# Hash attention and an MLP in one kernel: the opening with the first chunk's attention alone, one PSUM bank a head, hash bits compared into place

## The chip, the cores and the metric

The kernel runs on one core of one Trainium2 chip. The metric is device time in microseconds (us), as the median of the runs. Engines are named as in the profile: PE (TensorE, with PEld for its weight loads), DVE (VectorE), ACT (ScalarE), POOL (GpSimd) and SP (SyncE). PEclk is the share of its clock that PE was granted.

## The reference, cut to what matters

There are 4 batches of 8 heads with 768 tokens of 64 dimensions, all in fp32. Each query and each key is hashed to 6 bits, and a query sees only the keys with the same 6 bits. The attention's output is laid out as rows of 512 and goes through a layer norm and an MLP of 2048 hidden units, with a residual.

```python
q_bits = (np.einsum('bhsd,dk->bhsk', q, proj) > 0)          # proj: 64 x 6
k_bits = (np.einsum('bhsd,dk->bhsk', k, proj) > 0)
mask = q_bucket[:, :, :, None] == k_bucket[:, :, None, :]
scores = np.where(mask, scale * q @ k.T, -1e9)
attn = softmax(scores) @ v
x = attn.transpose(0, 2, 1, 3).reshape(B, S, H * D)         # 768 x 512 a batch
out = x + np.maximum(layernorm(x) * g @ w_ch1, 0) @ w_ch2   # 512 -> 2048 -> 512
```

## The kernel before, in words

**Operands.** For each head, `slots` holds queries and keys transposed: rows 0 to 63 are the 64 dimensions in bf16, rows 64 to 69 are the six hash bits as +24 or -24 (batch 0: +0.5 or -0.5, with the operands scaled down to match). One product of 70 rows then gives the score with the mask already in it: each bit that differs takes so much off the score that its exponential is as good as nothing. `vaug` holds the values with a column of ones, so that the value product gives the denominator too. A tiny multiple of the values' sum is added for queries that match no key; for batch 0 it comes into PSUM by "opener" products with the constant tile `epsk` (L431).

**Chunks, units and steps.** Work goes in 12 chunks of 256 queries: three a batch, `(b, t)`. A chunk has four head pairs, and a pair three units of four (head, key block) products each. A unit has a score step (four products, L406, and one exponential of 128x1024 on ACT, L412) and a value step (eight products of 65 columns, L440; the last of a pair divides by the denominator on DVE, L455 and L465). Each chunk then goes through its MLP: norm (L484 to L501: DVE statistics, normalised rows `xn`, and `rs` on POOL), a transpose of `xn` (on PE, L509, for the first two chunks), eight up steps (L522, 8 products of 256 columns each, ReLU by DVE and ACT in turn) and eight down steps (L535, 4 products of 512 columns each).

**Preparation of q and k.** From batch 1 on, transposes and hashes are made from bf16 copies by DMA transposes and 32x32 DVE transposes (`narrow`, `blocks`, `operands`, `hashes`), planned as fillers between attention steps. Batch 0 has no time for that: its heads go through PE (`transposes`, L211: three blocks of q and three of k a head, each block two key or query blocks high). DVE evicts and scales q (L219), ACT evicts k (L221), both to `qkT` in fp32, and `casts` copies them to `slots` (L226 to L231, POOL, ACT or DVE). `hash_pair` hashes two heads' q or k by four products of 32 columns that lie side by side in PE (L306), compares them to bits on DVE (L311), and copies the bits to their rows in `slots` (L322 to L326). Because a transposed block holds the tokens of two key blocks, batch 0's blocks lie in another order in `slots`, which `CMAP` undoes.

**What sets the order.** The first two chunks are written out by hand in `first_two` (L643 to L703): the units of chunk 0 and chunk 1 alternate by head pair, and the dictionary `also` names what is issued between them.

```python
groups = [(0, 0), (0, 1), (1, 0), (1, 1), (2, 0), (3, 0), (2, 1), (3, 1)]
seq = [(n, 3 * j + g) for j, n in groups for g in range(3)]
...
18: [mlp[0][0][1]],
22: [mlp[0][3]],
23: [mlp[0][1][0][1], lambda: nxt.blocks(0, 1, 0), lambda: nxt.blocks(0, 1, 1)],
```

So the first MLP's norm comes behind unit 18, its transpose behind unit 22 and one of its eight up steps behind unit 23; the other seven are fillers of the third chunk's stage. From the third chunk on, `interleave` spreads fillers by their costs between the units: the down steps of the chunk before the previous one, the preparation steps of the string `plan`, and the up steps of the previous one. Every engine takes its own instructions strictly in order; where one waits, all behind it on that engine wait. PE is kept busy ahead of the first data by products with a constant (`keep_awake`, L652: 26, 3 and 10 of them). PSUM holds two score tiles (`ps_sc`, two banks each), two banks for `av` (`ps_av`) and two for everything else (`ps_mm`), among them the batch 0 transposes.

**Loads.** q and k of batch 0 go out on SP and ACT, proj on ACT behind both (L152), values on SP; POOL issues w1 (L559), w2 (L566) and all loads of batch 1.

Of the kernel before, what the change touches and what calls it, by code (L numbers as in the profile page):

```python
# [9 lines left out]
F32 = mybir.dt.float32  # L10
# [10 lines left out]
Q_SCALE = 2.0**-12  # L21

# [6 lines left out]
def kernel(  # L29
# [11 lines left out]
    nc = tc.nc  # L41
# [24 lines left out]
    proj1 = consts.tile([P, 2, 32], F32)  # L66
# [26 lines left out]
    CMAP = [[2 * i + par for par in range(2) for i in range(HC)]] + [list(range(NC))] * (B - 1)  # L93
# [10 lines left out]
    for i in range(2):  # L104
# [12 lines left out]
        tc.tile_pool(name="ps_av", bufs=2, space=bass.MemoryType.PSUM)  # L117
# [18 lines left out]
    def load_half(b, half):  # L136
# [7 lines left out]
        for lo, hi in zip(cuts, cuts[1:]):  # L144
            for nm, src in (("q", q), ("k", k)):
                eng = nc.gpsimd if b == 1 else nc.scalar if nm == "k" and hi - lo == 1 else nc.sync
                eng.dma_start(
                    out=t[nm][:, lo:hi],
                    in_=src[b, h0 + lo : h0 + hi].rearrange("h (p c) d -> p h c d", p=P),
                )  # L150
        if b == 0 and half == 0:
            nc.scalar.dma_start(out=proj1[0:D, 0, 0:n_bits], in_=proj)  # L152

# [19 lines left out]
    class Prep:  # L173
# [24 lines left out]
        def tokens(self, h, par):  # L198

            return self.sl[0:D, h, :, par * HS : (par + 1) * HS]  # L200

        def transposes(self, h, a):

            if a == 0:
                self.qkT[h] = work.tile([P, 2, HS], F32, tag="qkT", bufs=4, name="qkT")
            if h == 1:
                tp = ps_sc.tile([P, 2, 512], F32, tag="sc", name="tpose")[:, 0, 0:HS]
            else:
                tp = ps_mm.tile([P, HS], F32, tag="mm", name="tpose")
            for i in range(HC):  # L210
                nc.tensor.transpose(  # L211
                    tp[:, i * P : (i + 1) * P],
                    self.tiles[h // 4]["qk"[a]][:, h % 4, 2 * i : 2 * i + 2].rearrange(
                        "p c d -> p (c d)"
                    ),
                    identf,
                )
            if a == 0:
                nc.vector.tensor_scalar_mul(self.qkT[h][:, a, :], tp, Q_SCALE)  # L219
            else:  # L220
                nc.scalar.activation(self.qkT[h][:, a, :], tp, AF.Copy)  # L221

        def casts(self, h):
            src = self.qkT[h]
            if h < 2:
                nc.gpsimd.tensor_copy(self.tokens(h, 0), src[0:D])  # L226
                nc.scalar.activation(self.tokens(h, 1), src[D:P], AF.Copy)
            else:
                eng = nc.gpsimd if h in (4, 6) else nc.vector
                eng.tensor_copy(self.tokens(h, 0), src[0:D])  # L230
                nc.vector.tensor_copy(self.tokens(h, 1), src[D:P])  # L231
# [67 lines left out]
        def hash_pair(self, j, a):  # L299

            if a == 0:
                self.pair_bits = work.tile([P, 2, HS], BF16, tag="bits", name="bits")
            bits = self.pair_bits
            hp = ps_mm.tile([P, HS], F32, tag="mm", name="hash")
            for g in range(4):
                nc.tensor.matmul(  # L306
                    hp[32 * g : 32 * (g + 1), :],
                    proj1[:, g % 2, :],
                    self.qkT[2 * j + g // 2][:, a, :],
                )  # L310
            nc.vector.tensor_scalar(  # L311
                bits[:, a, :], hp,
                scalar1=0.0, scalar2=0.5, op0=AOP.is_gt, op1=AOP.subtract,
            )
            if a == 0:
                return
            for g in range(4):
                par = g % 2
                dst = self.sl[D:K1, 2 * j + g // 2, :, par * HS : (par + 1) * HS]
                src = bits[32 * g : 32 * g + n_bits]  # L320
                if g == 2 and j == 0:
                    nc.scalar.activation(dst, src, AF.Copy)  # L322
                elif g == 3:
                    nc.gpsimd.tensor_copy(dst, src)
                else:
                    nc.vector.tensor_copy(dst, src)  # L326

# [60 lines left out]
    def att_units(b, t, x):  # L388
# [3 lines left out]
        q0 = t * CT  # L392
        for j in range(NP):
# [7 lines left out]
            for g, grp in enumerate(groups):  # L401

                def scores(grp=grp, g=g, state=state):
                    sc = ps_sc.tile([P, 4, CT], F32, tag="sc", name="sc")
                    for i, (h, kj) in enumerate(grp):
                        nc.tensor.matmul(  # L406
                            sc[:, i, :],
                            sl[0:K1, h, 1, kj * P : (kj + 1) * P],
                            sl[0:K1, h, 0, q0 : q0 + CT],
# [9 lines left out]
                def values(grp=grp, g=g, state=state, j=j, ha=ha):  # L419
                    if g == 0:  # L420
                        av = ps_av.tile([P, 2, TT, D1], F32, tag="av", name="av")
                        state["av"] = av
                        opens = []
                        if b == 0:
                            opens = (
                                [va[:, ha : ha + 2, c, :] for c in range(NC)]
                                if (t, j) == (0, 0)
# [10 lines left out]
                    for i, (h, kj) in enumerate(grp):  # L438
                        for qi in range(TT):
# [3 lines left out]
                                va[:, h, CMAP[b][kj], :],  # L443
# [29 lines left out]
    def mlp_steps(b, t, x):  # L473
# [56 lines left out]
        def down(i, part):  # L530
# [8 lines left out]
            if part == 3:  # L539
# [5 lines left out]
                    out=out[b].rearrange("(p c) d -> p c d", p=P)[:, CMAP[b][t * TT + i], :],  # L545
# [92 lines left out]
    def head(h):  # L638
        prep.transposes(h, 0)
        prep.transposes(h, 1)  # L640
        prep.casts(h)

    def first_two():  # L643
# [6 lines left out]
        nc.sync.dma_start(out=gbc, in_=moe_g_ln.partition_broadcast(P))  # L650

# [4 lines left out]

        keep_awake(26)
        head(0)
        head(1)
        nc.vector.tensor_copy(proj1[D : 2 * D, 1, 0:n_bits], proj1[0:D, 0, 0:n_bits])  # L660
        keep_awake(3)
        prep.hash_pair(0, 0)
        prep.hash_pair(0, 1)
# [279 lines left out]
```

## Time and profile before

| | |
|---|---|
| runs: median (lowest to highest) | 328.85 us (328.68 to 329.95) |
| profiled execution: span from the first to the last instruction | 329.9 us |
| mean granted PE clock over the span | 0.967 |
| PE busy (PEld) | 310.5 us, 94% (228.3) |
| ACT, DVE, POOL busy | 215.3, 185.9, 84.5 us |
| moved by DMA | 40.93 MB, mean 124 GB/s |
| chain that ended last | PE 79%, DVE 7%, ACT 7%, DMA 2% |

The profile is of one execution; its span agrees with the slowest of the runs and lies 1.05 us above their median. In the groups by line, each row names the line, the engine, the operation, output<-input, the shape and the count, then the busy time and the mean duration of one in ns, then the idle time of the engine just before them and what ended it. In the timeline, a row has the start and the duration in us; a bracket shows the idle time ahead of it and its releaser. In the windows view, each row has a stretch, its length, then the busy time of PE, PEld, DVE, ACT and POOL with the number of instructions, then the granted PE clock, the DMA share and GB/s. PE's records overlap, since products are pipelined: how long a step holds PE is read from start to start, not from the durations.

### The profile page before, as it was taken

What the parts mean: (1) busy time and instruction counts of PE and PEld (TensorE: products, weight loads), DVE (VectorE), ACT (ScalarE), POOL (GpSimd) and SP (SyncE); (2) the same over time, 40 slices, a digit from 0 to 9 for tenths busy, and PEclk for the clock granted to TensorE, in tenths of its full rate; (3) what the DMA queues carried; (4) which work ended last, traced back from release to release, by engine and by line L of the source; (5) the groups of instructions that cost most, each with busy time, mean ns of one, the idle gap of its engine ahead of it and who ended that gap; (6) DMA issues with size and microseconds to landing.
All of it is one profiled execution on the core that took longest, in us unless ns stands there. A gap on an engine that the chain in (4) does not pass through costs nothing.

```text
span 329.9 us, 7872 instructions
## 1 busy us (share of the span) xinstructions
PE 310.5 (94%) x3276; PEld 228.3 (69%) x3276; DVE 185.9 (56%) x406; ACT 215.3 (65%) x269; POOL 84.5 (26%) x105
## 2 busy tenths in 40 slices
PE   7787899799999999999999999989999999999992
PEld 6654568665966967957867868748769678686650
DVE  2688773773394587365497585535533634546420
ACT  5574777643695795787795886897758667573110
POOL 4466424662130524054155030010100200201000
PEclk9999856799999999999999999999999999999999
DMA  7999996576549649669724834020020110200301
GB/s 249 354 223 298 233 295 133 115 158 176 144 98 234 159 155 182 160 129 289 177 59 103 102 75 93 1 67 34 0 66 34 31 67 2 64 34 2 98 3 68
DMA packets 64874, 40.93 MB, mean 124 GB/s; under 512 B 47184, under 2 KB 59728, under 8 KB 64832
## 3 DMA queue, kind: packets, MB, share of 16 engines
q1 hardware_dynamic: 60368, 31.85, 39.3%
q0 software_dynamic: 4096, 8.13, 10.3%
q8 instruction: 27, 0.44, 0.6%
q10 hardware_dynamic: 368, 0.39, 0.3%
q14 instruction: 15, 0.12, 0.1%
HBM read 27.98 MB, written 6.88 MB: 106 GB/s over the span
## 4 chain that ended last, share of the span: by engine, by line
PE 79%; DVE 7%; ACT 7%; DMA 2%; issue 2%; ACTq 0%; SPq 0%; DVEq 0%
PE hp L522 25%; PE o L535 20%; PE sc L406 17%; PE av L440 10%; ACT ex L412 4%; PE hash L275 3%; DVE slots L326 2%; PE hash L306 2%; DMA proj<-in_proj_dram 1%; ACT knat L191 1%; ACT qnat L191 1%; DMA xnT<-xn 1%; PE tpose L211 1%; DVE stats L484 1%; DVE bits L311 1%
## 5 line engine op out<-in xcount | busy, mean ns | idle before, releaser
L412 ACT ACTIVATE ex<-sc,expb 128x1024 bf16<-128x1024 f32 x144 | 159.8, 1114 | 69.4 <-PE sc L406 69.0
L522 PE MATMUL hp<-xnT,w_sb 128*128 128x256 bf16 x768 | 100.5, 276 | 2.4 <-DVE hbuf L129 1.7
L535 PE MATMUL o<-w_sb,hbuf 128*128 128x512 bf16 x384 | 96.0, 379 | 0.2
L406 PE MATMUL sc<-slots 70*128 70x256 bf16 x576 | 91.8, 282 | 2.9 <-DVE slots L326 2.9
L522 PEld LDWEIGHTS <-w_sb 128*128 128x128 bf16 x768 | 72.7, 99 | 12.0 <-issue 2.1
L440 PEld LDWEIGHTS <-ex 128*128 128x128 bf16 x1152 | 55.6, 100 | 22.1 <-ACT ex L412 8.2
L406 PEld LDWEIGHTS <-slots 70*128 70x128 bf16 x576 | 53.0, 100 | 17.5 <-DVE slots L326 2.7
L440 PE MATMUL av<-vaug,ex 128*128 128x65 bf16 x1152 | 61.8, 197 | 2.2 <-ACT ex L412 2.2
L129 DVE TENSOR_SCALAR hbuf<-hp 128x512 bf16<-128x512 f32 x48 | 33.1, 690 | 53.7 <-PE hp L522 52.9
L535 PEld LDWEIGHTS <-hbuf 128*128 128x128 bf16 x384 | 35.5, 97 | 28.6 <-issue 0.6
L500 POOL TENSOR_SCALAR rs<-mv 128x2 f32<-128x2 f32 x12 | 5.7, 477 | 172.6 <-DVE mv L485 172.6
L133 ACT ACTIVATE hbuf<-hp 128x512 bf16<-128x512 f32 x48 | 28.5, 594 | 24.2 <-PE hp L522 24.2
L540 DVE SCALAR_TENSOR_TENSOR x<-o,rs,x 128x512 f32<-128x512 f32 x24 | 17.8, 741 | 36.8 <-PE o L535 36.8
L465 DVE TENSOR_TENSOR x<-x,rc 128x256 f32<-128x256 f32 x36 | 20.6, 573 | 1.0
L486 DVE SCALAR_TENSOR_TENSOR xn<-x,mv,gbc 128x512 bf16<-128x512 f32 x24 | 18.3, 782 | 0.3 <-DVE mv L485 0.3
L457 DVE TENSOR_SCALAR rc<-av 128x4 f32<-128x4 f32 x36 | 5.7, 158 | 18.6 <-PE av L440 18.6
L484 DVE BATCH_NORM_STATS2 stats<-x 128x6 f32<-128x512 f32 x24 | 15.4, 678 | 0.2
L458 DVE TENSOR_TENSOR x<-av,vsum 128x256 f32<-128x256 f32 x36 | 14.9, 414 | 0.0
L330 POOL CAST vaug<-vnat 128x1536 bf16<-128x1536 f32 x8 | 12.0, 1498 | 9.3 <-PE av L440 4.9
L191 ACT ACTIVATE knat<-knat 128x768 f32<-128x768 f32 x16 | 13.5, 846 | 0.0
L191 ACT ACTIVATE qnat<-qnat 128x768 f32<-128x768 f32 x16 | 13.5, 844 | 0.0
L501 POOL TENSOR_TENSOR rs<-rs,mhalf 128x2 f32<-128x2 f32 x12 | 12.7, 1061 | 0.6
(80 smaller groups left out, 207.6 us busy)
## 6 DMA issues: line engine op xcount, KB each, us to landing
out_dram<-x SPq DMA_DIRECT2D x24, 256.0 KB
vnat<-in_v_dram SPq DMA_DIRECT2D x7, 768.0 KB
qnat<-in_q_dram SPq DMA_DIRECT2D x11, 384.0 KB
knat<-in_k_dram SPq DMA_DIRECT2D x11, 384.0 KB
w_sb<-in_moe_w_ch_dram POOLq DMA_DIRECT2D x4, 1024.0 KB, 13.2
slots<-slots SPq DMA_DIRECT2D x6, 384.0 KB
qnat<-in_q_dram POOLq DMA_DIRECT2D x2, 768.0 KB, 12.9
knat<-in_k_dram POOLq DMA_DIRECT2D x2, 768.0 KB, 14.5
```

The costliest lines, as they stand in the source:

```text
L129: nc.vector.tensor_scalar_max(dst, src, 0.0)
L133: nc.scalar.activation(dst, src, AF.Relu if relu else AF.Copy)
L191: nc.scalar.activation(src, src, AF.Square, accum_out=sq[:, a, col : col + 1],)
L406: nc.tensor.matmul(sc[:, i, :], sl[0:K1, h, 1, kj * P : (kj + 1) * P], sl[0:K1, h, 0, q0 : q0 + CT],)
L412: nc.scalar.activation(ex, sc, AF.Exp, bias=expb[:, 1:2] if b else expb[:, 0:1], scale=scale if b else scale / Q_SCALE,)
L440: nc.tensor.matmul(av[:, h - ha, qi, :], state[g][:, i, qi * P : (qi + 1) * P], va[:, h, CMAP[b][kj], :], start=(b > 0 and (g, i, qi) == ( ...
L465: nc.vector.tensor_tensor(xv, num, rc.unsqueeze(3).to_broadcast([P, 2, TT, D]), op=AOP.mult)
L484: nc.vector.bn_stats(stats, x[:, i, :])
L486: nc.vector.scalar_tensor_tensor(xn[:, :, i, :], x[:, i, :].rearrange("p (o d) -> p o d", d=P), mv[:, i, 0:1], gbc.rearrange("p (o d) -> p ...
L522: nc.tensor.matmul(hp[:, i, :], w1_sb[:, dt, nt * P : (nt + 1) * P], st["xnT"][:, dt, :], start=(dt == 0), stop=(dt == ND - 1),)
L535: nc.tensor.matmul(o2, st["h"][:, nt, i * P : (i + 1) * P], w2_sb[:, nt, :], start=(nt == 0), stop=(nt == NH - 1),)
L540: nc.vector.scalar_tensor_tensor(x[:, i, :], o2, st["rs"][:, i : i + 1], x[:, i, :], op0=AOP.mult, op1=AOP.add,)
```

## The change

- The first chunk's twelve units now come first, alone, with all of batch 0's transposes, casts and hashes between them; then the second chunk's twelve, with the whole norm, transpose and all eight up steps of the first chunk's MLP between them. The third chunk's stage no longer has seven of these up steps.
- A head's three k blocks and the one q block that the first chunk needs are transposed to one PSUM bank and evicted by one instruction with the square root of the old scale (2^-6 for both). The other two q blocks come later, for two heads together (`late_transposes`).
- A head is hashed by one product of 64 columns over 512 (its two column groups hold the bits of the two stacked blocks), and the compares on DVE write the bits directly into `slots`. `hash_pair` and its copies go.
- `ps_av` has one bank each of two names, `av0` and `av1`. The transposes use `av1`, and the first chunk's `av` tiles all use `av0`; later chunks alternate.
- All four pairs of the first chunk open with six products of `vaug` instead of one of `vsplit` (before: the first pair alone).
- proj is loaded ahead of the second head's k; the 3 and 10 wake products go; `CMAP` goes, since blocks are found by `key_block` and `query_blocks`.

```diff
-        ps_av ... tc.tile_pool(name="ps_av", bufs=2, space=bass.MemoryType.PSUM)
+        ps_av ... tc.tile_pool(name="ps_av", bufs=1, space=bass.MemoryType.PSUM)
...
+        def transposes(self, h, engine):
+            tp = ps_av.tile([P, 4, P], F32, tag="av1", name="tpose")
+            t = self.tiles[h // 4]
+            for i in range(HC + 1):
+                src, c = (t["k"], 2 * i) if i < HC else (t["q"], 0)
+                nc.tensor.transpose(
+                    tp[:, i, :],
+                    src[:, h % 4, c : c + 2].rearrange("p c d -> p (c d)"),
+                    identf,
+                )
+            self.scaled(h, tp, engine)
...
+        def scaled(self, key, tp, engine):
+            self.qkT[key] = work.tile([P, 4, P], F32, tag="qkT", bufs=4, name="qkT")
+            if engine is nc.scalar:
+                nc.scalar.activation(self.qkT[key], tp, AF.Copy, scale=HALF_SCALE)
             else:
+                engine.tensor_scalar_mul(self.qkT[key], tp, HALF_SCALE)
...
+        def hash_bits(self, key):
+            hp = ps_mm.tile([P, 4, P], F32, tag="mm", name="hash")
+            nc.tensor.matmul(
+                hp[D : 2 * D].rearrange("p c t -> p (c t)"),
+                proj1,
+                self.qkT[key].rearrange("p c t -> p (c t)"),
+            )
+            for par in range(2):
+                r0 = D + 32 * par
+                nc.vector.tensor_scalar(
+                    self.places(key, slice(D, K1), par),
+                    self.as_placed(key, hp[r0 : r0 + n_bits]),
+                    scalar1=0.0, scalar2=0.5, op0=AOP.is_gt, op1=AOP.subtract,
+                )
...
                     if g == 0:
-                        av = ps_av.tile([P, 2, TT, D1], F32, tag="av", name="av")
+                        slot = 0 if (b, t) == (0, 0) else (j + 1) % 2
+                        av = ps_av.tile([P, 2, TT, D1], F32, tag=f"av{slot}", name="av")
...
-                                if (t, j) == (0, 0)
+                                if t == 0
...
         keep_awake(26)
-        head(0)
-        head(1)
-        nc.vector.tensor_copy(proj1[D : 2 * D, 1, 0:n_bits], proj1[0:D, 0, 0:n_bits])
-        keep_awake(3)
-        prep.hash_pair(0, 0)
-        prep.hash_pair(0, 1)
-        keep_awake(10)
+        head(0, act, (pool, dve))
+        dve.tensor_copy(proj1[D : 2 * D, 32 : 32 + n_bits], proj1[0:D, 0:n_bits])
+        head(1, act)
+        bits(0)
+        head(2, act)
+        bits(1)
+        S(0)
+        load_w1()
+        head(3, dve)
         prep.values(0)
+        S(1)
+        bits(2)
+        V(0)
+        head(4, act)
+        S(2)
+        V(1)
+        bits(3)
+        S(3)
+        V(2)
+        head(5, dve)
+        nxt.load(0)
...
+        S(8)
+        late(0, act, in_av)
+        V(7)
+        bits(7)
+        S(9)
+        V(8)
+        load_w2()
+        late_bits(0)
+        S(10)
+        V(9)
+        late(1, act, in_av)
+        prep.split_sums(0)
+        S(11)
+        V(10)
+        late_bits(1)
+        S(12)
+        V(11)
...
+            0: [norm[1]],
+            1: [lambda: late(2, dve, in_mm), lambda: late_bits(2)],
+            2: [lambda: prep.split_sums(1), lambda: nxt.load(1), lambda: nxt.load_v(0)],
+            3: [lambda: late(3, dve, in_mm), lambda: late_bits(3), xtrans],
+            4: [ups[0][1], lambda: nxt.narrow(0, 0)],
+            5: [ups[1][1], lambda: nxt.narrow(0, 1)],
...
+            11: [ups[7][1]],
+        for u in range(n0):
+            S(n0 + u + 1)
+            for f in also[u]:
+                f()
+            V(n0 + u)
...
-        fillers = (mlp[0][1][1:] if n == 2 else []) + [norm]
+        fillers = [norm]
```

Here `head(h, ...)` is the transposes and casts of head h, `bits(h)` its hash, `late(j)` and `late_bits(j)` the same for the two late q blocks of heads 2j and 2j + 1, and `S(u)` and `V(u)` the score and value step of unit u.

## The prediction

> **What bounds the kernel now.** I read the windows view first, cut where the granted clock changes, then the timeline of the opening, then the groups by line.
>
> ```profile
> core 0: us, PE busy (x) PEld busy (x) DVE busy (x) ACT busy (x) POOL busy (x), PEclk, DMA share, GB/s
> 9.50:31.40 21.90, 17.28 (x196) 11.62 (x197) 17.02 (x31) 13.95 (x16) 13.83 (x15) 1.00 1.10 293
> 31.40:34.80 3.40, 3.40 (x25) 3.01 (x25) 2.00 (x5) 1.61 (x2) 1.41 (x2) 0.50 1.24 207
> 34.80:41.60 6.80, 5.76 (x78) 3.28 (x76) 5.62 (x11) 4.95 (x5) 2.92 (x3) 1.00 1.21 249
> 41.60:55.30 13.70, 13.40 (x115) 9.96 (x114) 7.23 (x15) 9.66 (x9) 5.49 (x5) 0.50 0.88 215
> 55.30:62.10 6.80, 5.06 (x58) 4.41 (x57) 6.26 (x12) 6.64 (x13) 1.68 (x2) 1.00 0.67 130
> 62.10:65.50 3.40, 3.40 (x24) 2.58 (x23) 1.60 (x2) 0.34 (x1) 3.24 (x5) 0.50 0.44 94
> 65.50:92.00 26.50, 26.39 (x307) 19.42 (x305) 13.00 (x25) 13.39 (x15) 9.12 (x11) 1.00 0.61 156
> 92.00:302.00 210.00, 207.91 (x2297) 156.46 (x2295) 121.03 (x285) 157.73 (x200) 41.62 (x48) 1.00 0.40 95
> ```
>
> The reader is to see three regions. From 65.5 us to 302 PE is busy over 98% at full clock (PEclk 1.00); nothing in the change touches that work, it only begins earlier or later. Before 65.5 no engine is full, and PE runs at half clock for 3.4, 13.7 and 3.4 us. So the change is decided in the first 92 us: there the third chunk's attention ends, and the eighth up step of the second chunk's MLP beside it. Call S(u) and V(u) the score and value steps of unit u. Before, V(23), the last of the first two chunks, ends at 55.8 with one up step of the first MLP done; the stage of the third chunk lasts 36.2 us, to 92.0.
>
> The half clock comes after idle PE, in the timeline:
>
> ```profile
> 29.01 0.49 PE L211 MATMUL tpose<-identf,qnat 128*128 128x128 f32 x3
> 31.25 0.82 PE L211 MATMUL tpose<-identf,knat 128*128 128x128 f32 x3 [1.75 <-DVE vsplit L358]
> 59.23 0.60 PE L406 MATMUL sc<-slots 70*128 70x256 bf16 x4
> 61.58 1.40 PE L522 MATMUL hp<-xnT,w_sb 128*128 128x256 bf16 x8 [1.74 <-DVE hbuf L129]
> ```
>
> Each wait of 1.75 us is followed by transposes or ups at double length. The changes lie on a grid of 3.41 us (31.38, 34.80, 41.62, 55.28, 62.10, 65.52), which reaches back to 0.66. I summed in each 3.41 us how long PE really streams (spacing of successive starts: score 0.107 us, value 0.028, transpose 0.107). Streaming under 0.41 to 0.50 of a stretch gives half clock in the next; 0.56 and more keeps it full. With a score counted three quarters (70 of 128 rows) one border, 0.42 to 0.44 of full speed, sorts every stretch but the first, and says why 41.6 to 55.3 stayed at half: at half clock attention alone reaches at most 0.415. The stretch with the first ups left it.
>
> **Prices.** From the groups by line and the timeline:
>
> ```profile
> L311 DVE TENSOR_SCALAR bits<-hash 128x384 bf16<-128x384 f32 x8 | 4.4, 553 | 1.8 <-PE hash L306 1.7
> L219 DVE TENSOR_SCALAR qkT<-tpose 128x384 f32<-128x384 f32 x8 | 4.4, 555 | 6.9 <-PE tpose L211 6.8
> L221 ACT ACTIVATE qkT<-tpose 128x384 f32<-128x384 f32 x8 | 3.9, 491 | 4.3 <-PE tpose L211 4.2
> L326 DVE COPY slots<-bits 6x768 bf16<-6x768 bf16 x11 | 7.4, 674 | 0.3
> 10.43 1.47 POOL L330 CAST vaug<-vnat 128x1536 bf16<-128x1536 f32 x1 [0.34 <-DMA vnat<-in_v_dram]
> 11.95 0.84 PE L431 MATMUL av<-vaug,epsk 128*128 128x260 bf16 x6 [0.21 <-POOL vaug L330]
> ```
>
> PE occupancy, start to start: four scores 0.44, eight values 0.24, six openers (L431) 0.68, four transposes 0.43, an up step 0.875, a down step 0.87. An old hash group (four 32-column products side by side, 384 columns) held PE 0.88 us, 0.64 of it streaming. The new hash is one product of 64 columns over 512: 0.64 x 512/384 = 0.85, plus the same 0.24: 1.09 us. No row shows a 64-column product; the ends are 0.85 (no overhead) and 1.3, I take 1.09. Evictions over 512 in place of 384: DVE 0.69 us, ACT 0.60. One head's bits take two DVE compares, 1.38 us; the copies into place (L326, eleven at 0.67 on DVE, four on POOL) go. A POOL cast of 64x512 is 0.55 to 0.8 (820 ns and 1208 ns for 64x768), taken as 0.6.
>
> **Part 1, the first chunk alone.** Work of a head pair on PE: 2 x 0.43 + 2 x 1.09 + 0.68 + 3 x 0.44 + 3 x 0.24 = 5.76 us; ACT has 3 x 1.11 + 0.6, DVE about 4.0, so PE leads. The openers are six instead of one for pairs 1 to 3 (+1.7 us in all), hashing rises from 8 x 0.88 to 12 x 1.09 (+6 us). S(0) starts at about 9.4 as before (9.55): the chain is transpose 3.8, eviction, proj landing at about 6.2, hash, compares to 8.85; proj is issued half a us earlier (head 1's k behind it; its transposes wait for their bank till 5.2 anyway), and the copies and 13 wake products are gone. Behind S(0) stand 4 x 5.76, less three transposes and two hashes done (3.5), plus two late query groups (2 x 1.52), split sums 0.68 and S(12) 0.44: 23.7, so 33.1.
>
> Stall A adds 2.4. POOL's order is now casts of heads 0 to 2, the two w1 issues (0.87 each), casts of head 3, then the values cast. Head 3's casts wait for DVE's scaling, which stands behind head 1's compares (end 10.95): 11.65. Casts to 13.3, vaug to 14.9; V(0) waits for it (before: 11.95). Behind V(0) on PE wait head 4's transposes and S(2), so ACT runs dry too. Small waits, walked link by link, add 0.4 a pair: V(11) ends at 37.1. The av bank of this chunk is single, but the next opener comes a hash and a score after the last value, over 1.2 us against 0.6 of DVE: hidden.
>
> **Part 2, the second chunk with the first MLP.** PE: 12 x 0.44 + 12 x 0.24 + 0.44 + 2 x 1.52 + 0.68 + 0.45 + 8 x 0.875 = 19.8. Stall B: the norm (two times 0.68 + 0.18 + 0.75, and gaps: 3.3 us) stands on DVE ahead of the scaling of late group 2; it starts when chunk 0's last x is written, about 38.7, ends at 42.0, and the late hash, next on PE, starts at 42.8 with PE idle since 39.6: 3.2 us. The next late group waits 1.3, the first up 1.05 for xnT, small waits 0.6. End of V(23): 37.1 + 19.8 + 6.2 = 63.1, 7.3 later than before. DVE's 17.8 us and ACT's 15.1 fit beside. On POOL the loads of the second half of b=1 now stand behind rs, which waits for the norm: issued near 45 instead of 29.3. They land some 14 us later (page), before that stage ends: no cost; if late, narrow and T11 slip, with about 10 us of slack before the fourth chunk. w2 goes out near 32 instead of 25, first used after 63.
>
> **Part 3, the third chunk.** Seven ups leave (6.1 us). What stays is 26.1 us of PE work; the same mix ran at 26.39 of 26.50. I take 27.0, against 36.2: the 1.74 wait and the 3.4 us at half clock (1.7 lost), both in the part of the ups, go with them. Full-clock sum: 63.1 + 27.0 - 92.0 = -1.9.
>
> **The clock.** Stall A puts S(1) and one hash into 10.9 to 14.3: 0.34 of streaming, under the border, so half clock follows; and 4.08 to 7.49 holds 0.42 to 0.46 (0.57 before, with twelve transposes and three wakes). Behind A PE leads, so a half stretch costs 1.7; the mix reaches 0.43 to 0.49 at half clock if the 64-column hash counts fully, so it gets out after about two: 3.4. Stall B costs one such stretch and part of a second, partly hidden under DVE: 2.5. Sum: -1.9 + 5.9 = +4.0. The span of 329.9 becomes 333.9. The profiled span lies 1.05 above the median of the runs (328.85), so 332.9: **333**.
>
> The Trainium skill ("TensorE: Matmul & The Clock Gate", Part 1, and its table of rules) lets the clock fall only after an idle window of about 3.4 us and asks for no gaps over about 3 us. The two gaps of 1.75 us here, each with half clock behind it, speak against it. By that rule stall A would be free, and the second rival below would hold. The same page (Part 4) says that transposes do not count as busy; the stretch 31.4 to 34.8, filled over half by nine fp32 transposes, brought full clock back, so here they count. Without them the opening would be emptier still, toward the first rival.
>
> **Rivals.**
> - Stuck at half clock. If columns count as rows seem to, the hash (64 of 128) counts half; the opening then reaches 0.31 to 0.40 at half clock and stays there, as attention did at 41.6 to 55.3. PE streams 17.7 us from V(0) to V(11); twice that, less 1.5 of absorbed waits, is +16, so with B: 329.9 - 1.9 + 16 + 2.5 - 1.05 = 345.5; leaving halfway, 337. For it: the score's weight. Against: no row shows it of columns. Chance 0.25.
> - The clock holds, and the kernel is faster: 329.9 - 1.9 - 1.05 = 327.0, 324 if the norm's stall is shorter than walked. It decides at the stretch before 14.3: vaug ready by about 13.9 lifts it over the border. For it: stretches of 0.56 stayed full. Against: POOL's order. Chance 0.22.
> - It changes nothing: waits at half clock absorb (V(0) waits for POOL at either clock), 328 to 330. Chance 0.13.
> - Forecast, some half stretches at both stalls, 330 to 336: 0.40.
>
> Only differences over 0.5% (1.64 us) can be told from none. Of the second rival most lies below 327.2: faster 0.18, same 0.20, slower 0.62. The range is 326.5 to 345.
>
> **What would show it.** Right: V(0) behind vaug at 14 to 16 us, PEclk 0.5 from 14.3, a PE gap of about 3 us near 40 ended by DVE qkT, V(23) at 65 to 70, the third stage of about 27 us at full clock. Wrong: hash products spaced far from 1.09; PEclk 1.00 throughout the opening; or a third stage near 36 us, which would mean that its DMAs or squares, not the ups, set it.

## The result and the profile after

| | before | after |
|---|---|---|
| runs beside each other: median (lowest to highest) | 328.9 us (328.68 to 329.95) | **336.94 us** (335.03 to 338.29) |
| ratio of after to before, 95% interval | | 1.0257 (1.021 to 1.0303) |
| profiled execution: span; clock | 329.9 us; 0.967 | 334.0 us; 0.981 |

The ratios leave out slow runs, those over 1.5% above the kernel's fastest; before has seven of them among the 29 runs of the last group below.

The kernel got slower by 8.0 us. The forecast of 333 named the direction; it is too low by 3.9. The two profiled spans differ by 4.1 us, though, close to the 4.0 forecast. So there are two questions: where the 4.1 us are, and where the rest of the 8.0 is.

The windows view of after, cut at its changes of clock and at the ends of V(23) and of the 16th up step:

```profile
core 0: us, PE busy (x) PEld busy (x) DVE busy (x) ACT busy (x) POOL busy (x), PEclk, DMA share, GB/s
1.80:7.20 5.40, 2.78 (x25) 2.36 (x23) 0.89 (x2) 2.09 (x3) 1.44 (x5) 1.00 0.92 283
7.20:14.00 6.80, 5.63 (x12) 2.01 (x12) 1.38 (x2) 1.20 (x2) 2.08 (x4) 0.50 1.06 378
14.00:48.10 34.10, 28.00 (x249) 17.22 (x249) 21.41 (x38) 18.67 (x19) 18.91 (x27) 1.00 0.92 186
48.10:51.60 3.50, 3.50 (x30) 2.65 (x31) 2.19 (x4) 1.11 (x1) 2.67 (x4) 0.51 0.98 186
51.60:68.70 17.10, 15.39 (x187) 12.96 (x186) 10.84 (x19) 11.15 (x12) 6.98 (x6) 1.00 0.80 200
68.70:96.20 27.50, 26.23 (x315) 19.27 (x312) 16.80 (x30) 18.02 (x25) 12.56 (x16) 1.00 0.65 163
96.20:306.00 209.80, 207.78 (x2304) 156.53 (x2302) 120.90 (x285) 157.99 (x201) 42.63 (x49) 1.00 0.40 98
```

The last row is the old last row, 210 us with PE busy 99%: nothing was lost or won there. The third stage is 27.5 us at full clock. All that was lost lies before 68.7. Before, the clock fell late (31.4, 41.6 and 62.1); now it falls at 7.2, in the opening, and at 48.1. The timeline of PE names the waits:

```profile
4.02 0.52 PE L209 MATMUL tpose<-identf,knat 128*128 128x128 f32 x3
4.37 0.27 PE L209 MATMUL tpose<-identf,qnat 128*128 128x128 f32 x1
8.37 0.87 PE L209 MATMUL tpose<-identf,knat 128*128 128x128 f32 x3 [3.73 <-DMA knat<-in_k_dram]
...
9.39 1.97 PE L259 MATMUL hash<-qkT,proj 128*64 128x512 f32 x2
...
19.31 0.84 PE L453 MATMUL av<-vaug,epsk 128*128 128x260 bf16 x6 [2.11 <-POOL vaug L340]
...
47.02 1.07 PE L259 MATMUL hash<-qkT,proj 128*64 128x512 f32 x2 [2.99 <-DVE qkT L234]
53.15 1.07 PE L259 MATMUL hash<-qkT,proj 128*64 128x512 f32 x2 [0.85 <-DVE qkT L234]
56.43 1.03 PE L544 MATMUL hp<-xnT,w_sb 128*128 128x256 bf16 x8 [0.86 <-DVE xnT L535]
```

In the kernel before, head 1's transposes end by 6.2 and the first hash starts at 6.73:

```profile
5.72 0.49 PE L211 MATMUL tpose<-identf,knat 128*128 128x128 f32 x3
6.73 0.71 PE L306 MATMUL hash<-qkT,proj 128*32 128x384 f32 x4 [0.34 <-DMA proj<-in_proj_dram]
```

The reader is to see four things. In after, head 1's transposes wait 3.73 us for k, which the forecast did not have. The transposes and the hash behind that wait take 0.87 and 1.97 us: half clock. The openers of V(0) wait for POOL's cast of the values. And one late group waits 2.99 us for DVE, with half clock behind it (the windows row of 48.1).

Marks from the two traces (first product of V(0), last of V(11) and V(23), last of the 16th up step, each by its start), beside the walk of the prediction:

| us | before | after | walked |
|---|---|---|---|
| first hash | 6.73 | 9.39 | |
| S(0) | 9.55 | 14.16 | 9.4 |
| V(0), behind its openers | 12.63 | 19.99 | 15.6 |
| end of V(11) | in both chunks' mix | 41.51 | 37.1, with the clock 40.5 |
| end of V(23) | 55.78 | 68.68 | 63.1, with the clock 69.0 |
| 16th up step | 91.90 | 96.15 | 96.0 |

(Walked V(0) is the cast's end at 14.9 and 0.68 of openers.) The groups by line, for the prices:

```profile
L266 DVE TENSOR_SCALAR slots<-hash 6x512 bf16<-6x512 f32 x24 | 16.6, 692 | 18.9 <-PE hash L259 18.5
L251 POOL CAST slots<-qkT 64x512 bf16<-64x512 f32 x23 | 14.3, 621 | 20.9 <-ACT qkT L232 14.5 <-DVE qkT L234 5.8
L232 ACT ACTIVATE qkT<-tpose 128x512 f32<-128x512 f32 x7 | 4.2, 596 | 12.7 <-PE tpose L209 12.4 <-PE tpose L221 0.3
L234 DVE TENSOR_SCALAR qkT<-tpose 128x512 f32<-128x512 f32 x5 | 3.4, 686 | 0.1
```

### The profile page after: what moved, and what is told of

Same layout as the page of the kernel before. It is cut to its first block, busy times and chain, and to the rows that moved or that the text cites. A ratio compares the mean times of both kernels' runs of the same rounds, so it can differ in the third digit from the quotient of the medians.

```text
span 334.0 us, 7790 instructions
## 1 busy us (share of the span) xinstructions
PE 311.2 (93%) x3238; PEld 225.9 (68%) x3238; DVE 184.1 (55%) x399; ACT 212.9 (64%) x265; POOL 90.2 (27%) x120
## 4 chain that ended last, share of the span: by engine, by line
PE 78%; DVE 7%; ACT 6%; DMA 3%; issue 2%; POOL 2%; ACTq 0%; SPq 0%; DVEq 0%; POOLq 0%
PE hp L544 25%; PE o L557 18%; PE sc L427 17%; PE av L462 10%; PE hash L259 3%; ACT ex L433 3%; PE hash L314 2%; DMA knat<-in_k_dram 2%; ACT knat L192 1%; DVE xn L508 1%; PE tpose L209 1%; DVE stats L506 1%; ACT qnat L192 1%; DVE bt L283 1%; PE av L453 1%
## 5 line engine op out<-in xcount | busy, mean ns | idle before, releaser
L544 PE MATMUL hp<-xnT,w_sb 128*128 128x256 bf16 x768 | 98.9, 272 | 1.3 <-DVE xnT L535 0.9
L427 PE MATMUL sc<-slots 70*128 70x256 bf16 x576 | 87.9, 274 | 0.5 <-DVE slots L266 0.4
L462 PEld LDWEIGHTS <-ex 128*128 128x128 bf16 x1152 | 54.1, 98 | 20.3 <-ACT ex L433 7.9
L427 PEld LDWEIGHTS <-slots 70*128 70x128 bf16 x576 | 51.5, 98 | 19.2 <-issue 6.8
L462 PE MATMUL av<-vaug,ex 128*128 128x65 bf16 x1152 | 59.9, 194 | 2.4 <-ACT ex L433 2.4
L134 ACT ACTIVATE hbuf<-hp 128x512 bf16<-128x512 f32 x48 | 28.5, 594 | 18.4 <-PE hp L544 18.4
L562 DVE SCALAR_TENSOR_TENSOR x<-o,rs,x 128x512 f32<-128x512 f32 x24 | 17.8, 741 | 35.0 <-PE o L557 35.0
L266 DVE TENSOR_SCALAR slots<-hash 6x512 bf16<-6x512 f32 x24 | 16.6, 692 | 18.9 <-PE hash L259 18.5
L251 POOL CAST slots<-qkT 64x512 bf16<-64x512 f32 x23 | 14.3, 621 | 20.9 <-ACT qkT L232 14.5
L259 PE MATMUL hash<-qkT,proj 128*64 128x512 f32 x24 | 14.6, 693 | 3.8 <-DVE qkT L234 3.8
L278 POOL CAST nat<-qnat 128x1536 bf16<-128x1536 f32 x6 | 9.0, 1500 | 25.4 <-DMA qnat<-in_q_dram 19.6
L480 DVE TENSOR_TENSOR x<-av,vsum 128x256 f32<-128x256 f32 x36 | 14.9, 414 | 0.0
```

Of the source, the lines that this page charges most:

```text
L134: nc.scalar.activation(dst, src, AF.Relu if relu else AF.Copy)
L259: nc.tensor.matmul(hp[D : 2 * D].rearrange("p c t -> p (c t)"), proj1, self.qkT[key].rearrange("p c t -> p (c t)"),)
L427: nc.tensor.matmul(sc[:, i, :], key_block(h, kj), query_blocks(h),)
L462: nc.tensor.matmul(av[:, h - ha, qi, :], state[g][:, i, qi * P : (qi + 1) * P], va[:, h, kj, :], start=(b > 0 and (g, i, qi) == (0, 0, 0)) ...
L544: nc.tensor.matmul(hp[:, i, :], w1_sb[:, dt, nt * P : (nt + 1) * P], st["xnT"][:, dt, :], start=(dt == 0), stop=(dt == ND - 1),)
L562: nc.vector.scalar_tensor_tensor(x[:, i, :], o2, st["rs"][:, i : i + 1], x[:, i, :], op0=AOP.mult, op1=AOP.add,)
```

## The experiments

Each ran beside the kernel before; the three groups of runs had its median at 328.86, 328.94 and 328.92 us. The marks are those of the table above.

| kernel | first hash | V(0) | V(11) | V(23) | 16th up | median us | ratio (95%) |
|---|---|---|---|---|---|---|---|
| before, again | 8.56 | 14.19 | | 55.95 | 90.43 | 327.84 | 0.9978 (0.9936 to 1.002) |
| after | 9.39 | 19.99 | 41.51 | 68.68 | 96.15 | 336.94 | 1.0257 (1.021 to 1.0303) |
| proj back | 6.57 | 16.02 | 38.37 | 65.55 | 93.01 | 335.54 | 1.0222 (1.0164 to 1.0279) |
| late groups on ACT | 8.91 | 19.59 | 41.12 | 66.94 | 94.39 | 334.74 | 1.0186 (1.0107 to 1.0265) |
| values first | 9.18 | 16.99 | 38.61 | 66.98 | 94.45 | 334.54 | 1.0178 (1.0122 to 1.0234) |
| PE kept awake | 10.14 | 19.57 | 43.26 | 71.68 | 99.15 | 336.19 | 1.0203 (1.0146 to 1.026) |
| ups back | 9.65 | 19.91 | 43.04 | 67.97 | 102.67 | 341.83 | 1.0381 (1.0325 to 1.0437) |
| the three together | 6.95 | 14.80 | 36.41 | 60.76 | 88.23 | 327.99 | 0.9966 (0.9938 to 0.9995) |
| late group early | 8.37 | 16.92 | 40.51 | 61.40 | 88.25 | 325.62 | 0.9916 (0.9877 to 0.9955) |
| late group early, again | 7.08 | 14.77 | 38.36 | 59.24 | 86.01 | 325.52 | 0.9923 (0.9894 to 0.9951) |
| two hashes at once | 6.91 | 13.90 | 36.65 | 57.54 | 84.53 | 325.14 | 0.9895 (0.9864 to 0.9927) |
| proj on POOL | 7.05 | 14.68 | 38.27 | 59.16 | 85.92 | 325.24 | 0.9924 (0.9893 to 0.9955) |
| both of these | 7.01 | 14.67 | 37.42 | 58.31 | 84.94 | **324.33** | 0.9881 (0.9845 to 0.9918) |

**The kernel before, again.** No edit.

> The kernel before, once more, to see the span of each of its runs. Theory A: a run's device time holds about 2.15 us beyond its span (the changed kernel: 336.2 beside 334.0), so the runs of the kernel before, 328.7 to 330, have spans of 326.5 to 328, and the profiled execution of 329.9 was some 3 us longer than they are; my difference from the median (1.05) then had the wrong sign. Theory B: the runs have spans of 328 to 330 and the profiled one stands for them.

The median is the same. The profile is another one: span 328.3 instead of 329.9, and its time, 330.09, lies 1.8 us above its span. Every run listed has this gap: 1.8 us for before, 2.2 for after (334.0 and 336.2). So theory A holds: by this gap (an estimate) the first profiled execution of before, with a span of 329.9, took about 331.7 us, not 329.9, and lies 2.8 above the median. Behind 30 us its clock fell three times, for 20.5 us in all; in this profile it fell twice, at 34.2 and 44.4, for 13.7 us. Spread over the 29 runs of the last group, before takes 326.11 to 332.64 us.

**proj back behind head 1's k.**

```diff
-            if (b, half, lo) == (0, 0, 0):
-                nc.scalar.dma_start(out=proj1[0:D, 0:n_bits], in_=proj)
         if b == 0 and half == 0:
+            nc.scalar.dma_start(out=proj1[0:D, 0:n_bits], in_=proj)
```

> The changed kernel with proj's load put back behind the load of head 1's k on ACT's queue. Theory K (the 3.73 us wait of head 1's transposes for k is the cause of the gap between walk and trace): the transposes start by 5.8, V(0) near 15, V(11) near 37.5 instead of 41.3, and the time falls by 3.5 to 4.5, to 332.5 to 333.5. Rival C (the clock, as in my forecast): the stall ahead of V(0) now brings the half clock to 14 to 18 us, and the time falls by at most 1.

In the timeline of this kernel, the wait for k is gone, and the rest of the opening stands within 0.25 us of the walk (S(0) 9.4, vaug 14.9):

```profile
5.42 0.55 PE L208 MATMUL tpose<-identf,knat 128*128 128x128 f32 x3 [0.69 <-ACT qkT L231]
...
6.57 1.07 PE L258 MATMUL hash<-qkT,proj 128*64 128x512 f32 x2 [0.50 <-DVE proj L704]
...
8.16 1.07 PE L258 MATMUL hash<-qkT,proj 128*64 128x512 f32 x2
9.17 0.61 PE L426 MATMUL sc<-slots 70*128 70x256 bf16 x4
...
14.77 0.59 PE L452 MATMUL av<-vaug,epsk 128*128 128x260 bf16 x2 [2.55 <-POOL vaug L339]
```

What the early proj did is in the trace's DMA records. In the kernel before, all but a few of the 128 packets of head 1's k (1.5 KB each) move on ACT's queue by 4.5 us, while SP's queue moves 59 to 80 packets in half a us. In after, proj's 64 packets of 24 bytes come first: k starts shortly before 4.5 and its last packets move at 7.5 to 8. From 6.0 on SP's queue moves 99 to 112 in half a us: from 6.0 to 8.0 us ACT's queue moved 43 packets, SP's 415. That the early proj delays k is shown by the edit; that k's tail is slow because SP's queue is so full is read from these records and was not tested apart. The Trainium skill ("DMA: Bandwidth & Descriptors", "Queues, rings and completion order") says that each DMA engine takes the queue rows in turn and drains a whole packet of one, some 9 to 17 descriptors, before it switches. What the trace counts as packets are single records of 1.5 KB, so their shares, a tenth against nine tenths, neither confirm nor refute that rule.

V(0) now waits longer for vaug (2.55 for 2.11 us), with a stretch at half clock behind it (14.4 to 17.8), so of the 5.0 us won at S(0) 3.1 are left at the 16th up step. The medians differ by only 1.4, less than theory K's 3.5 to 4.5 and more than rival C's 1: this profiled execution was the fastest of its four. Its S(0) is the earliest of all, too. In the five profiles of kernels with proj behind k on ACT's queue, head 1's transposes start at 5.4 to 6.0 and S(0) at 9.2 to 13.2; in the four with proj ahead and no wake products between, at 7.9 to 8.6 and 13.3 to 14.2.

**Late groups 2 and 3 scaled by ACT.**

```diff
-            1: [lambda: late(2, dve, in_mm), lambda: late_bits(2)],
+            1: [lambda: late(2, act, in_mm), lambda: late_bits(2)],
-            3: [lambda: late(3, dve, in_mm), lambda: late_bits(3), xtrans],
+            3: [lambda: late(3, act, in_mm), lambda: late_bits(3), xtrans],
```

> The changed kernel with the two late query groups of the second chunk scaled by ACT instead of DVE, so that PE's late hash no longer stands behind the norm. Theory N: the waits of 2.99 and 0.85 us for DVE qkT go, the half clock at 48 to 52 with them, up 0 starts near 52 instead of 56.4: 3 to 5 us less, 332 to 334. Rival D: DVE's chain (norm, compares, sums, xnT) holds up 0 anyway and the late waits only hid it: 0 to 1.4 us less (the two scalings), 335.5 to 337.

The waits of 2.99 and 0.85 us became two of 1.31: ACT has three exponentials in a row ahead of the scaling.

```profile
41.16 3.24 ACT L433 ACTIVATE ex<-sc,expb 128x1024 bf16<-128x1024 f32 x3 [0.68 <-PE sc L427]
44.94 1.97 PE L259 MATMUL hash<-qkT,proj 128*64 128x512 f32 x2 [1.31 <-ACT qkT L232]
```

1.8 us are won at the 16th up step, 2.2 in the median, which lies between the theory's range and the rival's. Of the 2.2 some 0.4 are outside the spans: this kernel's runs last 1.8 us longer than their spans, after's 2.2; the runs don't show why. In the changed kernel the cause is plain in the timeline of DVE: the norm's two halves, then the scaling.

```profile
43.05 0.69 DVE L506 BATCH_NORM_STATS2 stats<-x 128x6 f32<-128x512 f32 x1
...
45.61 0.75 DVE L508 SCALAR_TENSOR_TENSOR xn<-x,mv,gbc 128x512 bf16<-128x512 f32 x1
46.28 0.68 DVE L234 TENSOR_SCALAR qkT<-tpose 128x512 f32<-128x512 f32 x1
```

**The values cast first.** `prep.values(0)` moves from behind `head(3, dve)` to ahead of `load_w1()`.

> The changed kernel with the cast of the first values issued on POOL ahead of w1's loads and of head 3's casts. Theory P: V(0) starts at 17.2, when the hash ahead of it ends, instead of 19.31, and the time falls by 2, to 335. Rival: head 3's casts, now 1.5 us later, hold S(4) and the gain is under 0.5.

The order on POOL in after shows what stood ahead of the cast, the two w1 issues and head 3's casts:

```profile
13.10 1.26 POOL L251 CAST slots<-qkT 64x512 bf16<-64x512 f32 x2 [1.67 <-ACT qkT L232]
14.32 1.74 POOL L581 DMA_DIRECT2D w_sb<-in_moe_w_ch_dram  x2
16.46 1.26 POOL L251 CAST slots<-qkT 64x512 bf16<-64x512 f32 x2 [0.41 <-DVE qkT L234]
17.79 1.47 POOL L340 CAST vaug<-vnat 128x1536 bf16<-128x1536 f32 x1
```

With the edit the openers have no wait for POOL, V(0) comes 3.0 us earlier; 1.7 are left at the 16th up step, since this execution's clock stayed at half for two stretches after stall B instead of one. The median falls by 2.4.

**PE kept awake through the wait for k.**

```diff
         head(0, act, (pool, dve))
+        keep_awake(64)
```

> 64 wake products are put between head 0's transposes and head 1's, so that PE streams while it waits for head 1's k; nothing else changes. Theory (the clock falls because PE stood idle 3.7 us there): head 1's transposes still start at about 8.4, but the stretch from 7.2 on stays at full clock; the first hash is spaced by 1.1 us instead of 1.97, the first value step starts 1.5 to 2.5 us earlier than in the changed kernel (19.99), and the 16th up at 93.7 to 94.7 instead of 96.15, if the later clock is the same. Rival (half clock there is hidden under the wait for data, as the waits on DMA and POOL end last): first value step within 0.5 us of 19.99.

The clock did what the theory said, and V(0) came where the rival said (19.57 for 19.99). The products fill the wait, and transposes and hashes behind them run at full clock; S(0) is 1.4 us earlier. But 64 products are too many: the last packets of head 1's k move between 7.0 and 7.5, and its transposes, in order behind the products, start at 9.60, which is 1.2 us later than in after.

```profile
5.04 4.72 PE L679 MATMUL wakep<-wake 128*128 128x128 bf16 x64
9.60 0.50 PE L209 MATMUL tpose<-identf,knat 128*128 128x128 f32 x3
...
18.32 1.46 PE L453 MATMUL av<-vaug,epsk 128*128 128x260 bf16 x6 [2.54 <-POOL vaug L340]
```

From head 1's transposes to the openers 8.7 us pass here (9.60 to 18.32) and 10.9 in after (8.37 to 19.31). So half clock in the opening makes that way 2.2 us longer, although POOL's cast ends last in both: the casts ahead of it on POOL wait for evictions, and these for transposes at half clock. Of what full clock wins here, 1.2 us are lost because the transposes start late behind the products, and 0.6 to half clock between the openers and V(0), which the longer wait for vaug brings. So the rival's number came, but not for its reason. That this execution's 16th up step is later than after's comes from half clock at 17.3 to 24.2 and 48.1 to 54.9; the medians are alike.

**Seven up steps back into the third stage.**

```diff
-            5: [ups[1][1], lambda: nxt.narrow(0, 1)],
+            5: [lambda: nxt.narrow(0, 1)],
...
-        fillers = [norm]
+        fillers = (mlp[0][1][1:] if n == 2 else []) + [norm]
```

> The changed kernel with ups 1 to 7 of the first MLP back in the third stage (up 0 stays beside the second chunk). Theory (the ups move work between stages, and that PE fills the third stage either way; they keep the second chunk's stretches above the border of the clock): the third stage grows from 27.5 to about 33.6 to 36, the second chunk shrinks by 6.1 us at full clock but falls to half clock for one or two stretches more, so the 16th up of the second MLP comes 0 to 3 us later than 96.15. Rival (beside the second chunk the ups stand in PE's way, in the third stage they hide in its waits): 2 us or more earlier than 96.15.

```profile
core 0: us, PE busy (x) PEld busy (x) DVE busy (x) ACT busy (x) POOL busy (x), PEclk, DMA share, GB/s
47.70:54.50 6.80, 5.96 (x33) 3.52 (x34) 3.32 (x8) 1.11 (x1) 4.46 (x7) 0.50 1.07 228
54.50:68.00 13.50, 10.16 (x130) 6.87 (x129) 8.48 (x14) 9.01 (x9) 6.27 (x6) 1.00 0.68 186
68.00:102.70 34.70, 32.51 (x376) 25.03 (x376) 17.57 (x35) 20.73 (x28) 14.64 (x17) 1.00 0.67 159
```

The third stage grows from 27.5 to 34.7 us. The second chunk, 27.2 us long with all eight ups, still takes 24.9 without the seven: PE is busy 10.2 of 13.5 us in the second row. The 16th up step is 6.5 us later, where the theory had 0 to 3 and the rival an earlier one. Of these, 1.5 were there at V(11), ahead of the moved steps; the other 5.0 came behind it. The median is 4.9 us above after's (341.83 against 336.94). So moving the seven up steps is worth about 5 us, and the loss lies in the rest of the change.

**The three single edits together.**

> proj's load goes back behind all of k, the values cast stands ahead of the w1 issues and of head 3's casts, and the late groups 2 and 3 of the second chunk are scaled on ScalarE. Theory (each of the three waits is a term of its own, -3.1, -1.7 and -1.8 us in the traces of the single edits at the 16th up): the 16th up starts at about 89.5 to 91 instead of 96.15, the time is 329 to 332. Rival (the terms overlap: the wait for the values is only there because the others moved it, and the clock takes back what is won): the 16th up at 92 to 93, the time 332 to 335.

The 16th up step is 7.9 us earlier than in after, more than the 6.6 that the three traces sum to, and the median is 8.9 lower against a sum of 6.0; both are better than the theory's range. The traces point to the clock: each single edit left at least one stretch at half clock in the second chunk, this profile has none behind 10.4 us. From V(11) to V(23) it takes 24.4 us, the kernel with the late groups on ACT alone, with the same two waits for ACT and 3.4 us at half clock, 25.8. With 327.99 us the kernel is 0.3% under before (0.05 to 0.6%): the three orders account for the whole loss. What is left are two waits for ACT and one for the norm:

```profile
40.24 1.07 PE L258 MATMUL hash<-qkT,proj 128*64 128x512 f32 x2 [1.31 <-ACT qkT L231]
45.23 1.07 PE L258 MATMUL hash<-qkT,proj 128*64 128x512 f32 x2 [1.31 <-ACT qkT L231]
48.52 1.03 PE L543 MATMUL hp<-xnT,w_sb 128*128 128x256 bf16 x8 [0.86 <-DVE xnT L534]
```

**Late group 2 ahead of the norm.** The kernel with proj back and the values first, and:

```diff
         late_bits(1)
+        late(2, act, in_mm)
         S(12)
+        late_bits(2)
         V(11)
...
-            1: [lambda: late(2, dve, in_mm), lambda: late_bits(2)],
+            1: [],
-            3: [lambda: late(3, dve, in_mm), lambda: late_bits(3), xtrans],
-            4: [ups[0][1], lambda: nxt.narrow(0, 0)],
+            3: [xtrans, lambda: late(3, act, in_mm)],
+            4: [ups[0][1], lambda: late_bits(3), lambda: nxt.narrow(0, 0)],
```

> As the kernel with all three edits, and the late query group 2 is transposed and hashed before the last value step of the first chunk, group 3 after the norm and scaled on ScalarE: no late group stands behind the norm on DVE. Theory (stall B of 2.99 us is the norm ahead of the scaling and hash on DVE, so that PE has nothing to do): no PE wait over 1.5 us near the end of the first chunk, no half clock between 40 and 56, the 16th up at 88 to 90, time 326.5 to 329.5. Rival (PE then waits for xnT instead, as the first up needs the same norm; the wait is only moved): 16th up within 1 us of the kernel with the three edits.

> The kernel with late group 2 ahead of the norm once more, beside the next two on one chip. Its runs came in two groups, near 325.2 and near 327.9, and its profile, a run of the later group, shows 2.29 us of PE waiting for proj. Theory (the groups are runs in which proj lands early or late): a profile near 325.2 shows the first hash near 6.6 instead of 8.37. Rival (the groups come from the clock's grid alone): the first hash is at 8.4 in such a profile too.

The median is 325.62, and 325.52 when run again: 11.4 us below after and 3.3 below before, a little better than the theory's 326.5 to 329.5. By its 16th up step the first profile is no earlier than the three edits together (88.25 for 88.23), which was the rival's sign; but its V(0) is 2.1 us later. From V(0) to that step it takes 71.3 us, the second profile 71.2, the three together 73.4. Of stall B one wait of 0.98 us is left:

```profile
43.70 0.40 PE L530 MATMUL xnTp<-ident,xn 128*128 128x128 bf16 x4 [0.98 <-DVE xn L507]
```

Its first profile has V(0) 2.2 us later than the second, because proj landed late there (2.29 us of PE wait for it). That did not explain the two groups of its times, as the next but one shows.

**Two hashes side by side.** `hash_two` puts one head's product into columns 0 to 63 of PE and the other's into 64 to 127, for heads 2 and 3, 4 and 5, 6 and 7.

> Three pairs of heads have their hash products side by side in one PSUM tile, each with 64 columns of PE, instead of one after the other. Theory (PE leads the opening, and products in different halves of PE's columns run beside each other, as the four of 32 columns did before the change): the two products take about 1.1 us together, 3 x 1.07 = 3.2 us leave PE, the last value step of the first chunk ends 2 to 3.5 us earlier after the first value step, time 322 to 324. Rival (they run one after the other, or the second head's scaling is waited for): within 1 us of the kernel without it (325.6).

```profile
11.88 1.40 PE L259 MATMUL hash<-qkT,proj 128*64 128x512 f32 x4
13.21 0.85 PE L470 MATMUL av<-vaug,epsk 128*128 128x260 bf16 x6
...
22.63 0.42 PE L479 MATMUL av<-vaug,ex 128*128 128x65 bf16 x8 [0.62 <-ACT ex L450]
```

The first two products take 1.33 us together from start to start (11.88 to 13.21), the other pairs 1.52 and 1.51, instead of two of 1.01 each. So they run partly beside each other; the theory's 1.1 was too good. From V(0) to the end of V(11) 22.75 us pass instead of 23.59, which is 0.8 less and not 2 to 3.5, and PE now waits 0.62 us for an exponential: ACT is nearly as late. The 16th up step is 1.5 us earlier, but the medians (325.14 and 325.52) can't be told apart, as the rival had it.

**proj loaded by POOL.**

```diff
     nc.vector.memset(proj1, 0.0)
+    nc.gpsimd.dma_start(out=proj1[0:D, 0:n_bits], in_=proj)
...
-            nc.scalar.dma_start(out=proj1[0:D, 0:n_bits], in_=proj)
```

> proj is loaded by POOL as its first DMA, so it stands neither ahead of nor behind head 1's k on ACT's queue. Theory (proj's landing makes the two groups of runs): the first hash starts by 6.7 in the profile, and the runs spread over less than 1.5 us, median 324.8 to 325.5. Rival (a POOL load comes late, or delays the identity that the first transposes need): first transposes or hash later than 6.7, time 326 to 328.

The first hash starts at 7.05, but no earlier than in the second profile without the edit (7.08), since in both the transposes run at half clock. The twelve times still spread from 324.42 to 327.75 us (324.13 to 327.08 without). So proj's landing doesn't make the spread; the theory fell. Of the five runs over 326.5 us in these two sets, four have a granted clock of 0.989 to 0.991 and one 0.997; the others have 0.991 to 0.998. So the clock has a part in the spread, but what sets it in a run was not settled.

**Both of these.**

> Both of the former: hashes of three head pairs side by side, proj loaded by POOL. Theory (PE leads, proj's landing makes the spread): 321.5 to 323.5 us, under both kernels. Rival (one of the two fails): 324.5 to 326.

The best kernel of the study, 324.33 us (323.35 to 324.67): 1.2% under before (0.8 to 1.6%). It lies between the theory's range and the rival's. It keeps the change's plan, with other orders, proj's load on POOL and hashes in pairs. Against the kernel with proj on POOL alone it is 0.9 us better, which the intervals don't settle.

## Why the prediction was wrong, by its steps

Two steps failed. The one that made the number is the last, from the profiled span to the median: it took 1.05 us off where 2.2 had to be added. The one in the walk is the start of S(0), where the delay of k was put at the half us of one issue. The span itself came out close (334.0 for 333.9), in part by luck, as the fourth point shows.

- **Prices: right.** Hash 1.01 start to start for 1.09 (6.57 to 7.58 and 8.16 to 9.17 with proj back); bits 692 ns (0.69), evictions 596 and 686 ns (0.60, 0.69), POOL casts 621 ns (0.6).
- **"S(0) starts at about 9.4 as before ... proj is issued half a us earlier (head 1's k behind it; its transposes wait for their bank till 5.2 anyway)": wrong**, 14.16. The wait for the bank was taken as the last one, and k's delay as the 0.5 us of one issue. Head 1's transposes start 3.0 us later than with proj back (8.37 for 5.42), and the way from them to S(0) takes 5.8 us, at half clock, for 3.8. With proj back, S(0) is at 9.17; other profiles with proj behind k have it at 9.9 to 13.2, so the 5.0 between these two is the largest difference that the profiles show.
- **Stall A: mechanism right.** With proj back, the openers start at 14.77 for a walked 14.9. In after they start at 19.31, since the delay of k, and half clock behind it, shift all that POOL has ahead of the cast.
- **The clock behind stall A, +3.4: wrong place.** In after the half clock came ahead of V(0), where it costs 2.2 us (by the kernel kept awake); behind V(0) full clock held to 48.15. The +3.4 stood in the sum for the 4.4 us by which V(0) was later than walked, so it was luck that V(11) came out near: 40.5 forecast, 41.51 measured. With proj back, where the walk up to stall A holds, the clock falls at 14.37 as forecast (14.3), but for one stretch of 3.41 us instead of two.
- **Stall B: right.** Waits of 2.99, 0.85 and 0.86 us for 3.2, 1.3 and 1.05, and one stretch at half clock. From V(11) to V(23) 27.2 us for 28.5.
- **Third stage: right.** 27.5 us at full clock for 27.0, and 34.7 when the ups are put back.
- **"The profiled span lies 1.05 above the median of the runs (328.85), so 332.9": wrong, and this is the miss.** A run's time is its span and 1.7 to 2.3 us. The span of 334.0, forecast as 333.9, is a time of 336.2; the step took 1.05 off where 2.2 had to be added, 3.2 us. The other 0.7 is the distance of after's profiled execution to its median (336.94). The same step hid that before's profile was of a long run (about 331.7). So 8.0 us between the medians are 4.1 between the spans, 2.8 for before's execution above its median, 0.7 for after's below its own, and 0.4 between the two gaps of span and time.
- **Rivals.** "Stuck at half clock" fell: the hash counts with its 64 columns. In after, PE works from 10.6 to 14.0 us at half clock without a gap, on four transposes and parts of two hashes. By spacings that is 0.45 of full speed if the hash counts fully, 0.29 if it counts half, and full clock followed; with proj back, the stretch from 4.1 to 7.5 has 0.48 or 0.36 and stayed full. Both fit the border of 0.42 to 0.44 only with the hash counted fully. The border is not sharp, though: by the same spacings the stretch from 17.4 to 20.8 of after has 0.41, and full clock followed. "The clock holds" fell as well. So did "waits absorb half clock": V(0) does wait for POOL at either clock, but the way from head 1's transposes to the end of POOL's cast is itself 2.2 us longer at half clock.
- **The page's rule of the clock.** The Trainium skill ("TensorE: Matmul & The Clock Gate", Part 1) lets the clock fall after an idle window of about 3.4 us. The traces disagree again: in after it falls at 48.15 behind a gap of 2.99 us, in the kernel with the late groups on ACT at 44.7, in a gap of 1.31.

What stays open: no profile shows a run of before near its median (327.1 of span), so where such a run saves 2.8 us against the one that was read is not known. Its granted clocks point to the half stretches: the run of 331.56 us has 0.967 as the profile has, the one of 326.3 has 0.993.

## What to carry to other kernels

When a step is moved, walk the transfers with it: with a load of 1.5 KB, 0.5 us to issue, ahead of it on its queue, head 1's k landed so late that its transposes started 2 to 3 us later, and half clock lengthened what stood behind that wait. On an engine that takes its work in order, put what others wait for (the values' cast, a late group's eviction) ahead of what has slack (weight issues, a norm); undoing three such orders turned a kernel 2.6% slower than before into one 0.3% faster, and with the late group ahead of the norm, proj's load on POOL and hashes in pairs the same plan became 1.2% faster. And before a span is turned into a time, ask what lies around it and whether the profiled execution is like the others.

## What the runs showed of the hardware

The row of the granted clock can leave out a half clock before its first change. In the timeline of the second profile of before, the first transposes take 0.85 to 0.88 us, and in the first one 0.49 to 0.63, under the same PEclk of 1.00:

```profile
3.98 0.88 PE L211 MATMUL tpose<-identf,qnat 128*128 128x128 f32 x3
4.64 0.85 PE L211 MATMUL tpose<-identf,knat 128*128 128x128 f32 x3
```

Durations of equal products tell it. The stretches of 3.41 us lie otherwise in each run: the first change is at 31.38 in the first profile of before, at 34.19 in the second, and reckoned back to the start the grids begin at 0.66 and 0.05 us (0.36 in after, 0.71 with proj back). The prediction had walked its stretches on the grid of one profile. The Trainium skill ("TensorE: Matmul & The Clock Gate", Part 1) says that the window runs freely and that counts of slow products differ from run to run; the traces agree.
